# Weight strips of 256 columns, conversions of 768, a half-chunk start and one masked copy per unit, in a kernel of RWKV attention followed by a multiplicative feed-forward

The kernel runs on one core of one Trainium2 chip. The metric is the device time of one execution in microseconds (us). Engines are called as the profile calls them: PE is TensorE, PEld its weight loads, DVE is VectorE, ACT is ScalarE, POOL is GpSimd.

## The reference

```python
# r, k, v: (4, 8, 768, 48) float32; w, u: (8, 48)
for t in range(768):
    cur = einsum('bhd,bhe->bhde', u * k[t], v[t])
    y[t] = einsum('bhd,bhde->bhe', r[t], state + cur)
    state = w * state + einsum('bhd,bhe->bhde', k[t], v[t])
x = y as (3072 tokens, 384)
a, b = x @ w1, x @ w2            # w1, w2: (384, 1024)
out = ((a * b) @ w3) @ w_out     # w3: (1024, 1024), w_out: (1024, 384)
```

The four weight matrices arrive as 64-bit floats, and must be made fp32 on the chip.

## The kernel before

The first part works in 24 units: six chunks of 128 time steps, four batch rows each. A unit scales k and r by powers of w (`krs`, on DVE), transposes them (PE), multiplies all pairs of time steps of each head (`ps_a`, PE), puts the upper triangle into a table `AT` that already holds the diagonal (a masked copy on DVE, the diagonal on ACT), and multiplies the table and the state with v and r (`ps_y`, PE). The four units of a chunk give 512 tokens, in `xT`. The second part works by chunk: for each of eight groups of 128 columns a tile of `abt` is the product of `x @ w1` and `x @ w2` (function `ab`), w3 and w_out are folded into one matrix on the way (`fold`), and `o` multiplies it with the tiles.

A weight piece is converted by one ACT and six DVE instructions, the same for any width:

```python
nc.scalar.activation(out=power, in_=hi.bitcast(F32), func=ABS)
nc.vector.scalar_tensor_tensor(dst, power, 1.125 * 2.0 ** -15, hi.bitcast(F32), ALU.is_ge, ALU.mult)
nc.vector.tensor_scalar(tb, hb, 0x07FFFFFF, 3, ALU.bitwise_and, ALU.logical_shift_left)
nc.vector.scalar_tensor_tensor(hb, hb, 0xC0000000, tb, ALU.bitwise_and, ALU.bitwise_or)
nc.vector.tensor_scalar(pb, hb, 0xFF800000, None, ALU.bitwise_and)      # from here: the low word
nc.vector.scalar_tensor_tensor(t, lo, 2.0 ** -52, power, ALU.mult, ALU.mult)
nc.vector.tensor_add(dst, dst, t)
```

The pairs of a unit use two PSUM tiles of 128 x 512 fp32 (one bank each, as this text calls that size), and two masked copies:

```python
ps = [psA.tile([C, NP, C], F32, tag="a", name=f"ps_a{n}_{i}") for i in range(2)]
for p in range(NP):
    for i in range(2):
        nc.tensor.matmul(ps[i][:, p, :], lhsT=kT[n][rows(i), p, :], rhs=rT[n][rows(i), p, :], ...)
for i in range(2):
    nc.vector.copy_predicated(AT[n][:, i], later.bitcast(I32)[:, None, :].to_broadcast([C, NP, C]), ps[i])
```

The second part is spread over the units by a plan, one list for each chunk; a scheduler then orders the instructions of each engine:

```python
beside = [
    W12[0],                                              # w1, w2: first 512 columns
    merge(W12[1], AB(0, range(KH))) + AB(0, range(KH, KF)),
    merge(AB(1), WO + W3(range(3))),
    merge(AB(2, range(KH)), W3(range(3, KF))) + O(0) + AB(2, range(KH, KF)),
    merge(O(1) + O(2), AB(3)),
    merge(O(3), AB(4)),
]
```

The kernel's PSUM pools hold eight tiles of at most this size, in pairs: two for transposes, two for `ps_a` of the pairs, two for `ps_y` and the states, two for the second part.

## Time and profile before

| | before |
|---|---|
| time, median of 3 runs | 565.74 us (564.63 to 566.33) |
| span of the profiled execution | 562.7 us |
| PE busy, all of it | 539.0 us, 96% |
| first matmul of the second part | 46.53 us |
| last `ps_b` of chunk 0 ends | 109.27 us |
| first matmul of O(0) | 254.7 us |

The last rows of the table are marks for a race: where PE is full, the time at which it reaches a mark says how far one kernel leads the other. The second mark can be read in the timeline of PE (start, length, engine, line, operation): the eighth tile's last group ends where the next unit's transposes start.

```profile
106.69 2.74 PE L408 MATMUL ps_b<-xT,w 128*128 128x512 f32 x6
109.27 0.60 PE L295 MATMUL ps_kT<-ident,krs 128*128 128x128 f32 x4
```

### The profile page before, as it was taken

To read this page: it belongs to the slowest core of one execution; us is meant where nothing else is said; L and a number is where in the kernel's file an instruction comes from. 1 tells how busy PE (TensorE), PEld (TensorE's weight loads), DVE (VectorE), ACT (ScalarE), POOL (GpSimd) and SP (SyncE) were. 2 spreads that over 40 slices of the span, in tenths; PEclk is the share of its full clock that TensorE was granted. 3 is DMA by queue.
4 is the path that set the end of the run, shared out by engine and by line. 5 is a ranking of instruction groups with operands and counts; after the bars stand their busy time and mean duration, and the time that the engine had idled before them with its cause. 6 is when DMAs were issued, how large, how long until landed. Compare 5 with 4: busy or idle time off the path is not lost.

```text
span 562.7 us, 8088 instructions
## 1 busy us (share of the span) xinstructions
PE 539.0 (96%) x3304; PEld 307.2 (55%) x3304; DVE 255.5 (45%) x495; ACT 169.2 (30%) x400; POOL 3.6 (1%) x17
## 2 busy tenths in 40 slices
PE   3869999999999999999999999999999999999996
PEld 2656555455655565565645556555555555544453
DVE  5999999998674696840220414233211100001100
ACT  3745544454433263331211213122132110111010
POOL 2000000000000000000000000000000000000000
PEclk9969999999999999999999999999999999999999
DMA  7956543554233243220110202021010000000001
GB/s 161 227 134 160 153 112 90 149 170 132 43 115 77 76 120 97 57 43 21 50 29 14 57 14 57 15 57 30 16 29 14 1 15 14 29 28 0 0 16 47
DMA packets 84129, 37.52 MB, mean 67 GB/s; under 512 B 76273, under 2 KB 79474, under 8 KB 84082
## 3 DMA queue, kind: packets, MB, share of 16 engines
q1 hardware_dynamic: 84082, 36.91, 25.0%
q8 instruction: 28, 0.46, 0.3%
q14 instruction: 19, 0.16, 0.1%
HBM read 32.18 MB, written 4.72 MB: 66 GB/s over the span
## 4 chain that ended last, share of the span: by engine, by line
PE 90%; DVE 6%; DMA 1%; issue 1%; ACT 1%; SPq 0%; DVEq 0%; ACTq 0%
PE ps_o L414 22%; PE ps_b L408 22%; PE ps_a L403 22%; PE ps_w L267 7%; PE ps_a L307 5%; PE ps_y L363 4%; PE ps_y L355 3%; PE ps_kT L295 2%; PE ps_s L381 2%; PE ps_rT L295 2%; PE ps_w3T L263 1%; DVE t L238 1%; DVE AT L310 1%; DMA raw<-in_moe_w_dram 1%; DVE w L239 1%
## 5 line engine op out<-in xcount | busy, mean ns | idle before, releaser
L403 PE MATMUL ps_a<-xT,w 128*128 128x512 f32 x288 | 133.4, 597 | 0.7 <-DVE w L239 0.7
L409 DVE TENSOR_TENSOR abt<-ps_b,a 128x512 f32<-128x512 f32 x48 | 33.1, 691 | 221.8 <-PE ps_b L408 196.5
L408 PE MATMUL ps_b<-xT,w 128*128 128x512 f32 x288 | 132.5, 594 | 0.1
L414 PE MATMUL ps_o<-w,abt 128*128 128x384 f32 x384 | 127.2, 488 | 0.0
L414 PEld LDWEIGHTS ps_o<-w,abt 128*128 128x128 f32 x384 | 72.0, 190 | 49.2 <-issue 2.0
L408 PEld LDWEIGHTS ps_b<-xT,w 128*128 128x128 f32 x288 | 54.2, 190 | 67.1 <-issue 63.5
L403 PEld LDWEIGHTS ps_a<-xT,w 128*128 128x128 f32 x288 | 52.9, 190 | 56.8 <-issue 50.1
L289 ACT ACTIVATE AT<-ident,dg 128x128 f32<-128x128 f32 x192 | 59.1, 391 | 1.7 <-DVE dg L284 1.7
L405 ACT COPY a<-ps_a 128x512 f32<-128x512 f32 x48 | 28.0, 584 | 104.3 <-PE ps_a L403 104.3
L310 DVE COPY_PREDICATED AT<-later,ps_a 128x512 f32<-128x512 int32 x48 | 33.0, 730 | 31.2 <-PE ps_a L307 30.9
L417 ACT COPY osb<-ps_o 128x384 f32<-128x384 f32 x24 | 11.5, 479 | 108.7 <-PE ps_o L414 85.7
L267 PE MATMUL ps_w<-wo,w3T 128*128 128x384 f32 x128 | 43.1, 490 | 0.0
L307 PEld LDWEIGHTS ps_a<-rT,kT 64*128 64x128 f32 x384 | 25.9, 198 | 19.2 <-issue 11.3
L307 PE MATMUL ps_a<-rT,kT 64*128 64x128 f32 x384 | 31.7, 299 | 2.7 <-ACT rT L298 2.7
L367 ACT COPY xT<-ps_y 128x384 f32<-128x384 f32 x24 | 11.5, 478 | 74.3 <-PE ps_y L363 74.3
L231 ACT ACTIVATE power<-raw 128x512 f32<-128x512 f32 (+1 forms) x36 | 23.6, 655 | 31.5 <-DVE t L238 19.7
L267 PEld LDWEIGHTS ps_w<-wo,w3T 128*128 128x128 f32 x128 | 23.7, 190 | 15.7 <-ACT w3T L264 0.6
L363 PE MATMUL ps_y<-AT,vnat 128*32 128x128 f32 x768 | 29.1, 274 | 2.4 <-DVE AT L310 1.3
L298 ACT COPY kT<-ps_kT 128x512 f32<-128x512 f32 x24 | 14.0, 585 | 40.7 <-PE ps_kT L295 40.7
L363 PEld LDWEIGHTS ps_y<-AT,vnat 128*32 128x32 f32 x768 | 22.4, 110 | 5.2 <-DVE AT L310 2.5
L277 DVE TENSOR_TENSOR krs<-krin,pn_in 128x768 f32<-128x768 f32 x24 | 22.9, 956 | 3.8 <-ACT pn_in L179 2.8
L238 DVE SCALAR_TENSOR_TENSOR t<-raw,power 128x512 f32<-128x512 uint32 (+1 forms) x36 | 23.6, 655 | 0.2
(64 smaller groups left out, 339.1 us busy)
## 6 DMA issues: line engine op xcount, KB each, us to landing
raw<-in_moe_w_dram SPq DMA_DIRECT2D x28, 512.0 KB, 3.6
krin<-in_k_dram SPq DMA_DIRECT2D x24, 192.0 KB, 2.8
krin<-in_r_dram SPq DMA_DIRECT2D x24, 192.0 KB, 3.4
vnat<-in_v_dram SPq DMA_DIRECT2D x24, 192.0 KB, 2.8
out_dram<-osb SPq DMA_DIRECT2D x24, 192.0 KB, 1.9
raw<-in_moe_w_out_dram SPq DMA_DIRECT2D x8, 384.0 KB, 2.9
ub<-in_u_dram SPq DMA_DIRECT2D x1, 192.0 KB, 5.3
wucol<-in_w_dram SPq DMA_DIRECT2D x2, 0.8 KB, 1.9
```

The costliest lines, as they stand in the source:

```text
L231: nc.scalar.activation(out=power, in_=hi.bitcast(F32), func=ABS)
L238: nc.vector.scalar_tensor_tensor(t, lo, 2.0 ** -52, power, ALU.mult, ALU.mult)
L267: nc.tensor.matmul(ps, lhsT=w3T[:, kc, :], rhs=wo[kc], start=(kc == 0), stop=(kc == KF - 1))
L289: nc.scalar.activation(out=AT[n][:, i, p, :], in_=ident, func=COPY, scale=dg[:, h:h + 1])
L307: nc.tensor.matmul(ps[i][:, p, :], lhsT=kT[n][rows(i), p, :], rhs=rT[n][rows(i), p, :], start=True, stop=True)
L310: nc.vector.copy_predicated(AT[n][:, i], later.bitcast(I32)[:, None, :].to_broadcast([C, NP, C]), ps[i])
L363: nc.tensor.matmul(to(q, g), lhsT=vv[:, p, x:x + Q], rhs=AT[n][:, i, p, :], start=(not c and m < P // Q), stop=True, skip_group_check=True)
L403: nc.tensor.matmul(pa, lhsT=w1[:, q, js], rhs=xT[c][:, q, :], start=(q == 0), stop=(q == KM - 1))
L405: nc.scalar.copy(out=a, in_=pa)
L408: nc.tensor.matmul(pb, lhsT=w2[:, q, js], rhs=xT[c][:, q, :], start=(q == 0), stop=(q == KM - 1))
L409: nc.vector.tensor_mul(abt[c, j], pb, a)
L414: nc.tensor.matmul(po, lhsT=abt[c, j][:, b * C:(b + 1) * C], rhs=w34[:, j, :], start=(j == 0), stop=(j == KF - 1))
```

## The change

The intent is to let PE begin the second part earlier, in the stretch where it idles: with weights that are complete in strips of 256 columns, two tiles of chunk 0 can be computed for the first two batch rows before the other two exist. Wider conversions and one masked copy for two shall save DVE instructions. The core of the diff:

```diff
-    NIN, NV, NS, NRAW = 3, 3, 2, 3
+    NIN, NV, NS, NRAW = 3, 4, 2, 3
-    w1 = const.tile([P, KM, DF], F32)
+    w1 = const.tile([P, DF // STRIP, KM, STRIP], F32)      # STRIP = 256; w2 alike
+    ab_pieces = [(dst[:, z], src.rearrange("(q p) n -> p q n", p=P)[:, :, z * STRIP:(z + 1) * STRIP])
+                 for z in range(DF // STRIP) for dst, src in ((w1, moe_w1), (w2, moe_w2))]
...
-    load(0)
+    load(0, "kr")
+    landed = {0: fetch(ab_pieces[0])}
     (ub is loaded here)
-    landed = {0: fetch(ab_pieces[0])}
-    load(1)
+    load(0, "v")
+    load(1, "kr")
     landed[1] = fetch(ab_pieces[1])
+    load(1, "v")
...
-        psA = arm.enter_context(tc.tile_pool(name="psA", bufs=2, space=PSUM))
+        psA = arm.enter_context(tc.tile_pool(name="psA", bufs=1 if fast else 2, space=PSUM))
...
-                ps = [psA.tile([C, NP, C], F32, tag="a", name=f"ps_a{n}_{i}") for i in range(2)]
+                ps = psA.tile([C, 2, NP, C], F32, tag="a", name=f"ps_a{n}")
-                for i in range(2):
-                    nc.vector.copy_predicated(AT[n][:, i], ...to_broadcast([C, NP, C]), ps[i])
+                nc.vector.copy_predicated(AT[n].rearrange("s i p t -> s (i p) t"),
+                                          ...to_broadcast([C, H, C]), ps.rearrange("s i p t -> s (i p) t"))
...
+        def ab(c, j, ts=slice(0, NT)):                       # only the tokens ts; 17 abt tiles, not 20
...
+            [none, none, none, W12[0] + AB(0, range(0, 2), halves[0]), none, W12[1][:1], none,
+             AB(0, range(0, 2), halves[1]) + W12[1][1:] + AB(0, range(2, 4))],
+            [none, W12[2], none, AB(0, range(4, 6)), none, W12[3], none, AB(0, range(6, 8))],
             merge(AB(1), WO + W3(range(3))),
-            merge(AB(2, range(KH)), W3(range(3, KF))) + O(0) + AB(2, range(KH, KF)),
-            merge(O(1) + O(2), AB(3)),
+            merge(AB(2, range(1)), W3(range(3, KF))) + O(0) + AB(2, range(1, KF)),
+            O(1) + merge(O(2), AB(3)),
```

More of the change, by code (lines that the diff above doesn't have):

```diff
@@ L63 @@
     PIECE = 512
+    STRIP = 256
+    RAW = KM * STRIP
     W_LOW, W_HIGH = 0.6, 1.6
@@ L85 @@
     krs = [const.tile([C, 2, H, PAD], F32, name=f"krs{i}") for i in range(NS)]
-    raws = [const.tile([P, PIECE], U64, name=f"raw{i}") for i in range(NRAW)]
+    raws = [const.tile([P, RAW], U64, name=f"raw{i}") for i in range(NRAW)]
     st = [const.tile([P, NP, PD], F32, name=f"st{b}") for b in range(B)]
@@ L100, with load @@
     NU = len(units)
-    def load(n):
+    def load(n, which="krv"):
         if n >= NU:
@@ L106, in load @@
         ts = slice(c * C, (c + 1) * C)
-        nc.sync.dma_start(out=krin[n % NIN][:, 0], in_=k[b, :, ts, :].rearrange("h t d -> t h d"))
-        nc.sync.dma_start(out=krin[n % NIN][:, 1], in_=r[b, :, ts, :].rearrange("h t d -> t h d"))
-        nc.sync.dma_start(out=vnat[n % NV][:, :, :D], in_=v[b, :, ts, :].rearrange("h t d -> t h d"))
-    w1 = const.tile([P, KM, DF], F32)
-    w2 = const.tile([P, KM, DF], F32)
+        for nm, src, dst in (("k", k, krin[n % NIN][:, 0]), ("r", r, krin[n % NIN][:, 1]), ("v", v, vnat[n % NV][:, :, :D])):
+            if nm in which:
+                nc.sync.dma_start(out=dst, in_=src[b, :, ts, :].rearrange("h t d -> t h d"))
+    w1 = const.tile([P, DF // STRIP, KM, STRIP], F32)
+    w2 = const.tile([P, DF // STRIP, KM, STRIP], F32)
     w34 = const.tile([P, KF, DM], F32)
-    ab_pieces = [(dst[:, q, js], src[q * P:(q + 1) * P, js])
-                 for js in (slice(z * PIECE, (z + 1) * PIECE) for z in range(DF // PIECE))
-                 for q in range(KM) for dst, src in ((w1, moe_w1), (w2, moe_w2))]
+    ab_pieces = [(dst[:, z], src.rearrange("(q p) n -> p q n", p=P)[:, :, z * STRIP:(z + 1) * STRIP])
+                 for z in range(DF // STRIP) for dst, src in ((w1, moe_w1), (w2, moe_w2))]
     sent = [0]
@@ L126, in fetch @@
             return None
-        raw = raws[sent[0] % NRAW][:, :src.shape[1]]
+        _, m, n = src.shape
+        raw = raws[sent[0] % NRAW][:, :m * n].rearrange("p (m n) -> p m n", m=m)
         sent[0] += 1
@@ L225, in convert @@
                 return
-            n = src.shape[1]
-            lo, hi = (raw.bitcast(U32).rearrange("p (n z) -> p n z", z=2)[:, :, z] for z in range(2))
-            t, power = (work.tile([P, PIECE], F32, tag="cv", bufs=4, name=nm)[:, :n] for nm in ("t", "power"))
+            _, m, n = src.shape
+            lo, hi = (raw.bitcast(U32).rearrange("p m (n z) -> p m n z", z=2)[:, :, :, z] for z in range(2))
+            t, power = (work.tile([P, RAW], F32, tag="cv", bufs=3, name=nm)[:, :m * n].rearrange("p (m n) -> p m n", m=m)
+                        for nm in ("t", "power"))
             tb, hb, pb = t.bitcast(U32), dst.bitcast(U32), power.bitcast(U32)
@@ L248, in out_weight @@
             wo[c] = work.tile([P, DM], F32, tag="wo", bufs=KF, name=f"wo{c}")
-            weight((wo[c], moe_w_out[c * P:(c + 1) * P, :]))
+            weight((wo[c][:, None, :], moe_w_out[c * P:(c + 1) * P, None, :]))
         def w3_weight(j, z):
@@ L254, in w3_weight @@
             js = slice(z * PIECE, (z + 1) * PIECE)
-            weight((w3n[j][:, js], moe_w3[j * P:(j + 1) * P, js]))
+            weight((w3n[j][:, None, js], moe_w3[j * P:(j + 1) * P, None, js]))
         def fold(j):
@@ L279, in scale @@
                 nc.scalar.copy(out=krs[n % NS][:, :, :, :D], in_=kr)
-            ruk = work.tile([C, H, D], F32, tag="ruk", bufs=2, name=f"ruk{n}")
+            ruk = work.tile([C, H, D], F32, tag="ruk", bufs=1, name=f"ruk{n}")
             dg = work.tile([C, H], F32, tag="dg", bufs=2, name=f"dg{n}")
@@ L302, in pairs @@
             if fast:
-                ps = [psA.tile([C, NP, C], F32, tag="a", name=f"ps_a{n}_{i}") for i in range(2)]
+                ps = psA.tile([C, 2, NP, C], F32, tag="a", name=f"ps_a{n}")
                 for p in range(NP):
                     for i in range(2):
-                        nc.tensor.matmul(ps[i][:, p, :], lhsT=kT[n][rows(i), p, :], rhs=rT[n][rows(i), p, :],
+                        nc.tensor.matmul(ps[:, i, p, :], lhsT=kT[n][rows(i), p, :], rhs=rT[n][rows(i), p, :],
                                          start=True, stop=True)
-                for i in range(2):
-                    nc.vector.copy_predicated(AT[n][:, i], later.bitcast(I32)[:, None, :].to_broadcast([C, NP, C]), ps[i])
+                nc.vector.copy_predicated(AT[n].rearrange("s i p t -> s (i p) t"),
+                                          later.bitcast(I32)[:, None, :].to_broadcast([C, H, C]),
+                                          ps.rearrange("s i p t -> s (i p) t"))
                 return
@@ L396, in body @@
         abt = {}
-        def ab(c, j):
-            abt[c, j] = work.tile([P, NT], F32, tag="abt", bufs=2 * KF + KF // 2, name=f"abt{c}_{j}")
-            js = slice(j * P, (j + 1) * P)
+        def ab(c, j, ts=slice(0, NT)):
+            if (c, j) not in abt:
+                abt[c, j] = work.tile([P, NT], F32, tag="abt", bufs=2 * KF + 1, name=f"abt{c}_{j}")
+            z, js = j * P // STRIP, slice(j * P % STRIP, j * P % STRIP + P)
+            n = ts.stop - ts.start
             pa = psF.tile([P, NT], F32, tag="f", name=f"ps_a{c}_{j}")
             for q in range(KM):
-                nc.tensor.matmul(pa, lhsT=w1[:, q, js], rhs=xT[c][:, q, :], start=(q == 0), stop=(q == KM - 1))
+                nc.tensor.matmul(pa[:, :n], lhsT=w1[:, z, q, js], rhs=xT[c][:, q, ts], start=(q == 0), stop=(q == KM - 1))
             a = work.tile([P, NT], F32, tag="sa", bufs=2, name=f"a{c}_{j}")
-            nc.scalar.copy(out=a, in_=pa)
+            nc.scalar.copy(out=a[:, :n], in_=pa[:, :n])
             pb = psF.tile([P, NT], F32, tag="f", name=f"ps_b{c}_{j}")
             for q in range(KM):
-                nc.tensor.matmul(pb, lhsT=w2[:, q, js], rhs=xT[c][:, q, :], start=(q == 0), stop=(q == KM - 1))
-            nc.vector.tensor_mul(abt[c, j], pb, a)
+                nc.tensor.matmul(pb[:, :n], lhsT=w2[:, z, q, js], rhs=xT[c][:, q, ts], start=(q == 0), stop=(q == KM - 1))
+            nc.vector.tensor_mul(abt[c, j][:, ts], pb[:, :n], a[:, :n])
         def o(c, b):
@@ L419, in o, with AB @@
             nc.sync.dma_start(out=out[row:row + C, :], in_=osb)
-        def AB(c, js=range(KF)):
-            return [lambda c=c, j=j: ab(c, j) for j in js]
+        def AB(c, js=range(KF), ts=slice(0, NT)):
+            return [lambda c=c, j=j: ab(c, j, ts) for j in js]
         def O(c):
@@ L431, in first @@
             convert(ab_pieces[i], landed[i])
-        half = len(ab_pieces) // 2
-        W12 = [[lambda i=i: first(i) for i in range(z * half, (z + 1) * half)] for z in range(2)]
+        W12 = [[lambda i=i: first(i) for i in (2 * z, 2 * z + 1)] for z in range(DF // STRIP)]
         WO = [lambda c=c: out_weight(c) for c in range(KF)]
@@ L446, in body @@
         KH = KF // 2
+        halves = [slice(0, NT // 2), slice(NT // 2, NT)]
+        none = []
         beside = [
-            W12[0],
-            merge(W12[1], AB(0, range(KH))) + AB(0, range(KH, KF)),
+            [none, none, none, W12[0] + AB(0, range(0, 2), halves[0]), none, W12[1][:1], none,
+             AB(0, range(0, 2), halves[1]) + W12[1][1:] + AB(0, range(2, 4))],
+            [none, W12[2], none, AB(0, range(4, 6)), none, W12[3], none, AB(0, range(6, 8))],
             merge(AB(1), WO + W3(range(3))),
-            merge(AB(2, range(KH)), W3(range(3, KF))) + O(0) + AB(2, range(KH, KF)),
-            merge(O(1) + O(2), AB(3)),
+            merge(AB(2, range(1)), W3(range(3, KF))) + O(0) + AB(2, range(1, KF)),
+            O(1) + merge(O(2), AB(3)),
             merge(O(3), AB(4)),
@@ L461, in body @@
         for c in range(NCH):
-            done = 0
+            plan = beside[c]
+            if not isinstance(plan[0], list):
+                cuts = [len(plan) * m // (2 * B) for m in range(2 * B + 1)]
+                plan = [plan[cuts[m]:cuts[m + 1]] for m in range(2 * B)]
             for b in range(B):
@@ L465, in body @@
                 load(n + 2)
-                steps = []
                 if n + 1 < NU:
-                    steps += [lambda: (scale(n + 1), turn(n + 1))]
-                steps += [lambda: (n + 1 < NU and pairs(n + 1), output(n), update(n))]
-                for i, step in enumerate(steps):
+                    scale(n + 1)
+                    turn(n + 1)
+                for step in plan[2 * b]:
                     step()
-                    due = len(beside[c]) * (b * len(steps) + i + 1) // (B * len(steps))
-                    while done < due:
-                        beside[c][done]()
-                        done += 1
+                if n + 1 < NU:
+                    pairs(n + 1)
+                output(n)
+                update(n)
+                for step in plan[2 * b + 1]:
+                    step()
         for step in tail:
```

## The prediction

> **What bounds the kernel now.** I read the whole-page summary first: it says which engine is full over the span and where it is not.
>
> ```profile
> span 562.7 us, 8088 instructions
> ...
> PE 539.0 (96%) x3304; PEld 307.2 (55%) x3304; DVE 255.5 (45%) x495; ACT 169.2 (30%) x400; POOL 3.6 (1%) x17
> ...
> PE   3869999999999999999999999999999999999996
> ...
> DVE  5999999998674696840220414233211100001100
> ...
> PEclk9969999999999999999999999999999999999999
> ```
>
> PE is full in nearly every slice of 14 us; only the first three slices and the last one fall short. So the change can only win in the first 47 us, or must be judged by whether it opens new holes later. The row of DVE shows the other limit: DVE is full from the second slice to about 125 us, just where PE is not. PEclk dips in the third slice. Then I cut the span into five stretches (start:end, length, then busy us of PE, PEld, DVE, ACT, POOL with counts, clock, DMA share, GB/s).
>
> ```profile
> 0.00:12.00 12.00, 2.19 (x10) 1.85 (x11) 6.56 (x33) 3.32 (x5) 3.58 (x17) 1.00 0.75 153
> 12.00:47.00 35.00, 26.82 (x337) 20.89 (x337) 32.01 (x62) 20.48 (x56) 0.00 (x0) 0.85 0.76 180
> 47.00:104.00 57.00, 56.23 (x444) 30.36 (x443) 56.34 (x111) 29.02 (x74) 0.00 (x0) 1.00 0.50 129
> 104.00:250.00 146.00, 145.76 (x1011) 85.65 (x1010) 110.52 (x213) 58.93 (x134) 0.00 (x0) 1.00 0.35 97
> 250.00:562.70 312.70, 307.95 (x1507) 168.44 (x1506) 50.05 (x80) 57.45 (x134) 0.00 (x0) 1.00 0.09 25
> ```
>
> PE idles 9.8 us before 12 us, 8.2 us between 12 and 47, 0.8 and 0.2 us in the next two stretches. DVE has 0.7 us free in 47:104, but 35 us free in 104:250. The view of waits of PE names the releasers, and the timeline shows that busy time flatters the start: the same 16 pair products take 2.08 us at 38.07 us and 1.16 us at 43.05 us.
>
> ```profile
> PE ps_p L178 <- DVE both L172: 8.0, 1, 8.0
> PE ps_kT L295 <- DVE krs L277: 4.0, 3, 1.8
> PE ps_a L307 <- ACT rT L298: 2.7, 1, 2.7
> PE ps_y L363 <- DVE AT L310: 1.3, 3, 0.9
> ...
> PE ps_w3T L263 <- DVE w3n L239: 0.2, 1, 0.2
> ```
>
> ```profile
> 38.07 2.08 PE L307 MATMUL ps_a<-rT,kT 64*128 64x128 f32 x16 [2.69 <-ACT rT L298]
> ...
> 43.05 1.16 PE L307 MATMUL ps_a<-rT,kT 64*128 64x128 f32 x16
> 46.53 1.12 PE L403 MATMUL ps_a<-xT,w 128*128 128x512 f32 x2
> ```
>
> The last line is the first matmul of the second part. Counting PE's work before it at dense rates from the timeline (transposes 0.88 us a unit, pairs 1.1, y of the first chunk 1.0, state product 0.6, table transposes 0.88): 0.88 + 5 x 0.88 + 5 x 1.1 + 4 x 1.0 + 4 x 0.6, with 0.8 for the first state read, is 18.0 us in 46.5 us. PE has thus lost 28.5 us there. Some 12 us go before any input and table is ready, so some 16.5 us are what an earlier start of the second part could aim at.
>
> [...] From start to start in the timeline a two-input instruction took 0.47 us at 384 elements, 0.60 at 512 and 0.87 at 768, thus about 1.04 ns an element and 0.07 us fixed[...]; the trace has 0.33 us for the 512-element bit mask[...].
>
> **The change, part by part.** (1) Wider conversion pieces. One of 512 is six DVE instructions, 4 x 0.60 + 2 x 0.33 = 3.07 us, and there are 12 for w1 and w2: 36.8 us. One of 768 is 4 x 0.87 + 2 x 0.47 = 4.40 us, and there are 8: 35.2 us. DVE saves 1.6 us, all in its full stretch. w_out and w3 keep their sizes. (2) One copy_predicated of 1024 columns for two of 512: 1.24 us from start to start become about 1.14. Seven or eight units lie in the full stretch: 0.7 us. The price is that the next unit's pair products wait for the whole copy; they lie far enough apart. (3) The first strips of w1 and w2 are complete after two pieces (8.8 us of DVE) where the old order needed six (18.4 us) for 512 columns. Tiles 0 and 1 of chunk 0 can then start on the first two batches: 4 groups of 3 matmuls with 256 columns, about 5.1 us of PE work moved forward, and as much with the other half once unit 3 is done. PE's columns stay equal, as a group of six passes takes 2.58 us at 512 columns. The splitting adds only 12 products and two short DVE multiplies (4 x 0.33 against 2 x 0.60, +0.1 us). (4) A first strip loaded early. It puts 786 KB instead of 524 KB ahead of the second unit's k and r, whose r already kept DVE waiting 0.5 us; 0.26 MB at the 180 GB/s of the second stretch is 1.4 us more wait. The fourth v tile lets v loads go sooner; no wait of DVE or PE on v stands in the waits. (5) Later chunks: w3's last five rows now go beside one tile of chunk 2 instead of four. PE has less to do beside them, so DVE must keep up.
>
> Now DVE's queue in the changed order, from 10.65 us (its first krs), up to the last conversion of w2: krs 8 x 0.87 = 7.0; the three ruk/dg instructions of nine units and two of a tenth, 13.6; seven copy_predicated, 8.0; state updates of six units (0.7 each, and 0.47 twice), 5.1; eight conversions, 35.2; four half multiplies and four full ones, 3.7. The sum is 72.6 us, with 2 us of waiting for the second unit's input: 85.3 us. In the kernel before, the last w2 conversion ended at 91.1 us, but with an extra krs, copy_predicated and state update before it (3.3 us). DVE as such gains only 2 to 3 us; the order does the rest. Up to the krs of unit 8 come 5.3 us more (w_out's first piece, a ruk pair, a dg, a copy, a state update, the krs): 90.6 us. PE must wait for this krs, as the order has the transposes of unit 8 ahead of the tail of tiles 6 and 7. I get some 2 us of PE idleness there and as much for unit 6 at 68 to 70 us. Behind it PE has 13 us of work: 0.9 transposes, 0.4 y, 1.1 pairs, 0.6 state, 1.8 rest of a, three more groups of 2.7[...]. Chunk 0's eighth tile is thus done at about 105 us. In the kernel before, the timeline puts this end at 109.3 us, with the same units done. **The lead is about 4 us**, not the 16.5 of the idle time, because DVE, which makes every operand that PE would use, stays full.
>
> From there both are bound by PE. In the w3 stretch I set the changed order side by side: each row needs 2 x 3.07 = 6.1 us of DVE and 0.88 + 16 x 0.32 = 6.0 us of PE. DVE has to interleave units of 4.6 us. Three shared buffers for w3 rows and their transposes let a row start only when a fold two before is done. My sums give PE small waits at the last two rows, 0 to 1.5 us together. The later order of O(1), O(2) and AB(3) has full PE on both sides: zero. Seventeen abt tiles instead of twenty suffice, as O(0) ends before the eighteenth is written. Sum: 4 gained, about 0.8 given back: 3.2 us, 565.7 - 3.2 = 562.5 us.
>
> **The rivals.** (a) PE's holes close fully: up to 16 us, 550 us. For it speaks the size of the hole; against it DVE's nearly full row up to 125 us. It needs the half-chunk work to land exactly in waits that otherwise stay empty, and the units not to be held up. (b) The half-chunk work couples DVE's strict order to PE early: DVE's multiplies wait for cold matmuls, the recurrence slips, and the lead vanishes: 565 to 568 us. The clock view with 0.85 between 12 and 47 us speaks for it; against it, my tallies leave 0.5 to 2 us between PE's end and DVE's turn at most places. (c) DVE becomes the bound in the w3 stretch, having lost three tiles' worth of cover (15.6 us of PE): up to 5 us of waits on w3n, so 566 us. Against it stand DVE's 35 us free in 104:250. (d) The larger first strip delays unit 1: at most 2 us, 564.
>
> **Range and chances.** Centre 562.5. Up to 6 us of further gain if the waits for units 6 and 8 vanish; 4 to 5 us the other way if (b) or (c) come true. I take 556.5 to 566.5. Two per cent is 11.3 us: faster by so much needs two thirds of the whole hole, 0.05; slower by so much has no cause that I see, 0.02.
>
> **What would show it.** The first 256-column ps_a should start near 28 us and the first full one near 51; chunk 0's last ps_b should end at 103 to 107 us. PE idle in 12:47 should fall, but new waits of kT on krs should stand between 60 and 95 us, about 4 us. Conversion rows should read near 0.95 us at 768 (start to start 0.87) and copy_predicated near 1.25 us. Waits of ps_w3T on w3n should stay under 2 us. I am wrong if DVE has idle time of more than 3 us before 85 us, if the first O matmul comes after 240 us (at 254.8 before, less three tiles, 239 without a lead), or if PE waits for w3n by more than 3 us.

Cut from the text: one term of the sum, 1.5 us of PE for switches and a slow start, an estimate for which no measured numbers were given. With it the sum was 90.6 + 12.9 + 1.5 = 105.0 us for the end of chunk 0's eighth tile, the "about 105" that stands; without it, it comes to 103.5, a lead of 5.8 us and not "about 4", and a forecast of some 561 us and not 562.5. Three figures of parts 1 to 3 are for shapes that the kernel before does not have, and can be worked out from the rates in the text (1.04 ns an element and 0.07 us fixed; 0.33 us for the mask of 512): 0.47 us for the mask of 768 columns ((0.33 - 0.07) x 1.5 + 0.07 = 0.46), 1.14 us for the copy of 1024 (1.13) and 0.33 us for the multiply of 256 (0.34). They are estimates; the measured values are 0.47, 1.19 and 0.33 us. "Cold" means matmuls at a low granted clock: in the kernel before, the clock was 0.50 from 38.07 to 40.10 us, where the 16 pairs took 2.08 us, and 1.00 from 43.05 to 44.20 us, where they took 1.16.

## The result

The changed kernel took 563.12 us in the median of four runs (562.22 to 563.47), the kernel before 565.77 (564.63 to 566.33) beside it. The ratio is 0.9953, with an interval of 0.9933 to 0.9973. Ratios here are the mean time of one kernel's runs over that of the other's of the same rounds, so not quite the ratio of the medians. The gain of 2.65 us is real, as the interval lies below 1. The whole-page summary of the kernel after, to be read against the prediction's first fence:

```profile
span 560.0 us, 8068 instructions
...
PE 536.6 (96%) x3328; PEld 310.4 (55%) x3328; DVE 256.5 (46%) x449; ACT 168.9 (30%) x398; POOL 3.7 (1%) x18
...
PE   2879999999999999999999999999999999999997
...
DVE  6989999998765979520320304233111100001100
...
PEclk9889999999999999999999999999999999999999
```

PE's third slice is fuller, and DVE is about as full as before. The clock is better in the third slice (8 for 6) and lower in the second (8 for 9). By stages (start:end, length, busy us of PE, PEld, DVE, ACT, POOL with counts, clock, DMA share, GB/s):

```profile
12.00:47.00 35.00, 28.60 (x323) 22.78 (x323) 32.40 (x52) 21.62 (x58) 0.00 (x0) 0.90 0.87 195
47.00:104.00 57.00, 54.66 (x490) 33.15 (x489) 56.52 (x95) 27.96 (x69) 0.00 (x0) 1.00 0.50 124
104.00:250.00 146.00, 144.94 (x1019) 87.21 (x1018) 109.30 (x198) 57.95 (x133) 0.00 (x0) 1.00 0.36 98
```

PE's idle time fell from 8.2 to 6.4 us between 12 and 47 us, and rose from 0.8 to 2.3 and from 0.2 to 1.1 us in the next two stretches. What PE waits for (us in total, times, longest):

```profile
PE ps_kT L300 <- DVE krs L282: 5.1, 5, 1.8
PE ps_a L312 <- DVE AT L314: 2.2, 1, 2.2
PE ps_a L312 <- ACT AT L294: 2.1, 1, 2.1
PE ps_w3T L268 <- DVE w3n L244: 1.1, 2, 0.6
```

The first and last lines I had expected. The two in the middle are new: pairs that wait for a table `AT`. Pairs do not read `AT`; what they need is the PSUM tile that the copy into `AT` empties. The view puts one of them down to ACT, which wrote diagonals of a later table at that moment; but the wait ended at 19.50 us, 0.14 us after the end of the masked copy (18.07 to 19.36 us in DVE's timeline), so I read it as a wait for the copy as well. The timeline of PE shows the other wait, and the marks:

```profile
26.88 1.56 PE L411 MATMUL ps_a<-xT,w 128*128 128x256 f32 x6
...
33.86 1.12 PE L312 MATMUL ps_a<-rT,kT 64*128 64x128 f32 x8 [2.16 <-DVE AT L314]
34.91 2.79 PE L416 MATMUL ps_b<-xT,w 128*128 128x256 f32 x6
37.54 1.46 PE L411 MATMUL ps_a<-xT,w 128*128 128x256 f32 x6
...
92.91 0.66 PE L300 MATMUL ps_kT<-ident,krs 128*128 128x128 f32 x4 [1.07 <-DVE krs L282]
...
103.79 2.74 PE L416 MATMUL ps_b<-xT,w 128*128 128x512 f32 x6
...
236.92 13.49 PE L422 MATMUL ps_o<-w,abt 128*128 128x384 f32 x41
```

The second part starts at 26.88 us and not at 46.53. But at 33.86 PE has stood still for 2.16 us, and the group after it takes 2.79 us, where the same six matmuls take 1.46 three microseconds later: the clock had dropped (0.53 granted between 33.86 and 37.50 us, 1.00 from there to 40.00). DVE's timeline shows both ends of the knot:

```profile
32.43 1.29 DVE L314 COPY_PREDICATED AT<-later,ps_a 128x1024 f32<-128x1024 int32 x1
...
37.74 0.42 DVE L417 TENSOR_TENSOR abt<-ps_b,a 128x256 f32<-128x256 f32 x1 [1.39 <-PE ps_b L416]
...
91.89 0.96 DVE L282 TENSOR_TENSOR krs<-krin,pn_in 128x768 f32<-128x768 f32 x1
```

The masked copy ends at 33.72 us and lets PE go at 33.86; PE's slow group then makes DVE, the engine that is full, wait 1.39 us at 37.74. The last line is the krs of unit 8, for which PE waits at 92.91.

The marks: chunk 0 ends at 106.37 us (103.79 and 2.58), 2.9 us ahead of the kernel before. The first O matmul starts at 236.92; before it was 254.7 (the prediction's 254.8 is from the view of the critical chain), less three tiles of 2 x 2.58 us that now come after it, 239.2, thus 2.3 us ahead. The spans differ by 2.7 us. So the whole gain is made before 106 us, and neither lost nor added to later.

### The profile page after: what moved, and what is told of

Its sections match the earlier page's. It is cut to its first block, busy times and chain, and to the rows that moved or that the text cites. A ratio compares the mean times of both kernels' runs of the same rounds, so it can differ in the third digit from the quotient of the medians.

```text
span 560.0 us, 8068 instructions
## 1 busy us (share of the span) xinstructions
PE 536.6 (96%) x3328; PEld 310.4 (55%) x3328; DVE 256.5 (46%) x449; ACT 168.9 (30%) x398; POOL 3.7 (1%) x18
## 4 chain that ended last, share of the span: by engine, by line
PE 83%; DVE 12%; issue 2%; DMA 1%; SPq 1%; ACT 0%; DVEq 0%; ACTq 0%
PE ps_o L422 22%; PE ps_b L416 20%; PE ps_a L411 20%; PE ps_w L272 6%; PE ps_a L312 4%; PE ps_y L369 3%; PE ps_y L361 2%; PE ps_s L387 2%; PE ps_kT L300 1%; PE ps_rT L300 1%; DMA krin<-in_r_dram 1%; DVE t L243 1%; PE ps_w3T L268 1%; DVE w L244 1%; DVE w L237 1%
## 5 line engine op out<-in xcount | busy, mean ns | idle before, releaser
L417 DVE TENSOR_TENSOR abt<-ps_b,a 128x512 f32<-128x512 f32 (+1 forms) x50 | 33.5, 670 | 222.8 <-PE ps_b L416 197.0
L411 PE MATMUL ps_a<-xT,w 128*128 128x512 f32 (+1 forms) x300 | 133.8, 580 | 0.4 <-ACT xT L373 0.4
L416 PE MATMUL ps_b<-xT,w 128*128 128x512 f32 (+1 forms) x300 | 133.3, 581 | 0.2 <-DVE abt L417 0.2
L416 PEld LDWEIGHTS ps_b<-xT,w 128*128 128x128 f32 x300 | 57.5, 193 | 67.7 <-issue 64.3
L411 PEld LDWEIGHTS ps_a<-xT,w 128*128 128x128 f32 x300 | 55.2, 190 | 55.4 <-issue 50.9
L413 ACT COPY a<-ps_a 128x512 f32<-128x512 f32 (+1 forms) x50 | 28.4, 568 | 114.2 <-PE ps_a L411 114.0
L314 DVE COPY_PREDICATED AT<-later,ps_a 128x1024 f32<-128x1024 int32 x24 | 31.6, 1316 | 20.0 <-PE ps_a L312 19.8
L236 ACT ACTIVATE power<-raw 128x512 f32<-128x512 f32 (+2 forms) x32 | 22.8, 711 | 37.1 <-DVE w3n L244 16.6
L243 DVE SCALAR_TENSOR_TENSOR t<-raw,power 128x512 f32<-128x512 uint32 (+2 forms) x32 | 23.1, 722 | 0.5
```

What stands on the lines that cost most here:

```text
L314: nc.vector.copy_predicated(AT[n].rearrange("s i p t -> s (i p) t"), later.bitcast(I32)[:, None, :].to_broadcast([C, H, C]), ps.rearrange( ...
L411: nc.tensor.matmul(pa[:, :n], lhsT=w1[:, z, q, js], rhs=xT[c][:, q, ts], start=(q == 0), stop=(q == KM - 1))
L413: nc.scalar.copy(out=a[:, :n], in_=pa[:, :n])
L416: nc.tensor.matmul(pb[:, :n], lhsT=w2[:, z, q, js], rhs=xT[c][:, q, ts], start=(q == 0), stop=(q == KM - 1))
L417: nc.vector.tensor_mul(abt[c, j][:, ts], pb[:, :n], a[:, :n])
```

## The experiments

Twelve kernels were run in three calls. The kernel before ran beside each, with medians of 565.97, 564.75 and 564.79 us, so I compare ratios and give both. The changed kernel was timed in a call of its own, e1, e2, e6 and e7 together in one call on one chip, the others in two calls on another chip.

| kernel | median us | ratio to before | interval | profiled span |
|---|---|---|---|---|
| changed kernel | 563.12 | 0.9953 | 0.9933 to 0.9973 | 560.0 |
| e1: two pair tiles, two copies | 559.00 | 0.9874 | 0.9856 to 0.9892 | 557.2 |
| e2: no half chunks | 562.97 | 0.9945 | 0.9929 to 0.9960 | 560.6 |
| e10: e1 without half chunks | 561.50 | 0.9942 | 0.9922 to 0.9963 | 559.8 |
| e12: before, one copy | 564.55 | 0.9996 | 0.9979 to 1.0014 | 561.8 |
| e6: changed, light conversion | 559.20 | 0.9879 | 0.9859 to 0.9900 | 557.4 |
| e7: before, light conversion | 557.61 | 0.9849 | 0.9829 to 0.9870 | 556.2 |
| e11: e1, light conversion | 557.04 | 0.9861 | 0.9841 to 0.9882 | 555.2 |
| e9: strips converted in thirds | 565.89 | 1.0022 | 1.0005 to 1.0039 | 562.3 |
| e3: e1, old order of loads | 559.88 | 0.9909 | 0.9892 to 0.9927 | 558.5 |
| e4: e1, three v tiles | 559.11 | 0.9901 | 0.9881 to 0.9921 | 556.8 |
| e5: before, late plan | 565.63 | 1.0012 | 0.9995 to 1.0029 | 563.7 |
| e13: e1, two multiplies on POOL | 581.11 | 1.0275 | 1.0252 to 1.0298 | 579.3 |

The theory: DVE is full up to about 90 us (in the changed kernel it is busy for 56.5 of the 57 us from 47 to 104) and sets when PE gets its operands, so the gain is small, and the merged masked copy takes part of it back, through the pair tile. The rivals: the half-chunk start itself is worthless, or DVE's amount of work does not matter.

### e1: undo the merged copy

```diff
-        psA = ...(name="psA", bufs=1 if fast else 2, ...)
+        psA = ...(name="psA", bufs=2, ...)
-                ps = psA.tile([C, 2, NP, C], F32, tag="a", ...)
+                ps = [psA.tile([C, NP, C], F32, tag="a", ...) for i in range(2)]
-                nc.vector.copy_predicated(<all 1024 columns>)
+                for i in range(2):
+                    nc.vector.copy_predicated(AT[n][:, i], ..., ps[i])
```

> The changed kernel with the old pair products: two one-bank tiles and two copies of 512 columns for each unit, the rest of the change kept. Theory: in the changed kernel the one pair tile made PE wait 2.1 us at 17.4 us and 2.2 us at 31.7 us for the copy of the unit before, and [...]the next 256-column group took 2.63 instead of about 1.4 us. With two tiles the wait at 31.7 us goes, and the time falls by 1 to 2 us to about 561.5. Rival: DVE is the bound of this stretch; two copies cost it 0.05 to 0.1 us more for each unit, 0.5 us up to unit 8, and the waits on PE were slack: 563 to 564. The order of the queues may shift as well; I look for the 256-column ps_b at half clock in the timeline.

It took 559.00 us, ratio 0.9874, against 0.9953 with the merged copy. The difference of the ratios is 4.5 us; the medians differ by 4.1, the means of all spans by 3.7 (557.1 and 560.8). The two intervals do not touch. One part undone is thus worth more than the whole change had gained, and e1 beats both kernels. Its timeline of PE:

```profile
32.43 0.41 PE L368 MATMUL ps_y<-AT,vnat 128*32 128x128 f32 x4 [1.24 <-DVE AT L315]
...
34.68 0.93 PE L312 MATMUL ps_a<-rT,kT 64*128 64x128 f32 x10
35.62 1.56 PE L415 MATMUL ps_b<-xT,w 128*128 128x256 f32 x6
...
90.18 0.65 PE L300 MATMUL ps_kT<-ident,krs 128*128 128x128 f32 x4 [1.44 <-DVE krs L282]
```

At 32.43 PE waits too, but 1.24 us and not 2.16, the group that took 2.79 us takes 1.56 (the mean clock from 12 to 47 us is 0.95, against 0.90), and DVE has no wait for it: in the view of waits, DVE waits 0.2 us in all between 17 and 90 us, in the changed kernel 2.2. Unit 8 is reached at 90.18 and not at 92.91.

What waits at 32.43 is not the same work, though. It is the y matmuls, which read the table; in e1 they stand ahead of the next pairs, which start at 34.68 without a wait. DVE's timeline has the two copies 0.8 us earlier than the one copy of the changed kernel (32.43), and y starts when the first of them is done:

```profile
31.64 1.34 DVE L315 COPY_PREDICATED AT<-later,ps_a 128x512 f32<-128x512 int32 x2
```

So the edit changed the order of the queues along with the tile, and the share of each is not separated. Nor did it end every wait of the pairs: both forms give one unit the same two banks, and at 18.68 us the pairs of e1 still wait 1.8 us for a copy (2.1 in the changed kernel).

By the transposes of unit 5 e1 leads by 1.4 us (62.25 and 63.69 us), which goes with DVE's saved waits; the other 1.3 us come between there and unit 8, where the scheduler put fewer instructions of later units ahead of unit 8's krs (one pair of `ruk` multiplies and one w_out instruction less). That this order is the cause of the second 1.3 us is an inference. Also open is whether one wide copy out of two such tiles would do as well; no run tried it.

### e12: the merged copy in the kernel before

```diff
(on the kernel before)
-        psA = ...(name="psA", bufs=2, ...)
+        psA = ...(name="psA", bufs=1 if fast else 2, ...)
-                ps = [psA.tile([C, NP, C], F32, tag="a", ...) for i in range(2)]
+                ps = psA.tile([C, 2, NP, C], F32, tag="a", ...)
-                for i in range(2):
-                    nc.vector.copy_predicated(AT[n][:, i], ..., ps[i])
+                nc.vector.copy_predicated(<all 1024 columns>)
```

> The kernel before with one pair tile of two banks and one copy of 1024 columns, nothing else. Theory: the shared tile costs PE its waits in the first 47 us in this kernel too, because the pair products of unit n+1 are issued before or just after the copy of unit n: 1 to 4 us slower, 567 to 570. Rival: without half-chunk groups behind the pair products PE has nothing to lose there, and DVE saves 0.05 us a unit: 565 to 566.

The ratio is 0.9996. In the kernel before, the merged copy costs nothing and saves nothing. PE waits as long as 3.2 us for a copy there, but what waits is y, which reads the table; no pairs wait for the pair tile in this run, as y stands ahead of them in PE's queue:

```profile
19.93 1.08 PE L364 MATMUL ps_y<-AT,vnat 128*32 128x128 f32 x32 [3.19 <-DVE AT L309]
```

Also, the second part begins only at about 46 us in that kernel, so that the wait holds up none of it. That this is why nothing is lost is my reading; what the run shows is that the loss belongs to the combination.

### e2 and e10: no half chunks, with one pair tile and with two

```diff
-            [none, none, none, W12[0] + AB(0, range(0, 2), halves[0]), none, W12[1][:1], none,
-             AB(0, range(0, 2), halves[1]) + W12[1][1:] + AB(0, range(2, 4))],
+            [none, none, none, W12[0], none, W12[1][:1], none,
+             AB(0, range(0, 2)) + W12[1][1:] + AB(0, range(2, 4))],
```

> The changed kernel without the half-chunk start: tiles 0 and 1 of chunk 0 are computed whole after unit 3, everything else kept. Theory: the first halves (four groups, 5.1 us of PE work at full clock) fill holes of PE that DVE leaves before 47 us, and two later waits for krs give part back; without them the end moves by 2 to 4 us, to 565 to 567, so that the half-chunk start is nearly the whole gain. Rival: the gain comes from the strips and the cheaper conversions, which let the second part start earlier anyway, and the early halves only delay the recurrence: 562 to 564.

> Two pair tiles and two copies (as e1) and no half-chunk start (as e2). In e2 the half start was worth nothing (562.97 against 563.1), but there the pair tile held PE up. Theory: the half start is worth its moved work once the pair products no longer wait; without it the time is 2 to 4 us above e1's 559.0, 561 to 563. Rival: DVE's queue is full anyway and decides when w1 and w2 are ready, so the half start is worth nothing here as well: 558.5 to 559.5, and the gain of e1 is that of the strips and the cheaper conversions.

With the single pair tile, the half-chunk start is worth nothing: 0.9945 without it, 0.9953 with it. With two tiles it is worth 3.8 us by ratio: 0.9942 without it, 0.9874 with it (2.5 us by the medians). Read the other way, the merged copy costs nothing by ratio where there are no half chunks (0.9945 in e2, 0.9942 in e10; 1.5 us by the medians), although the pairs of e2 wait 1.9 and 2.2 us for it as in the changed kernel. By ratio, then, it is not these waits as such that cost, but what stands behind them. The timeline of PE in e10 shows what fills the gap in e1:

```profile
37.35 0.41 PE L368 MATMUL ps_y<-AT,vnat 128*32 128x128 f32 x4 [1.82 <-issue]
...
38.70 1.92 PE L368 MATMUL ps_y<-AT,vnat 128*32 128x128 f32 x28
```

Where e1 has three groups of 256 columns, from 35.62 to 39.7 us, e10 stands still for 1.82 us and then runs slowly (1.92 us for 28 y matmuls, 1.07 in e1 at 33.37). Slow matmuls do not follow every wait: after the 1.82 us here they were slow from 37.70 us on (14 state products took 1.08 us, 0.67 at 32.47), and after the 2.16 us in the changed kernel as well (2.79 us above), but after one of 2.38 us in e10 (before 28.55 us) four transposes took 0.66 us, as they do without a wait (0.65 at 25.08 us). What decides this is not shown.

### e6, e7, e11: half of the conversion left out

```diff
-        def convert(piece, raw):
+        def convert(piece, raw, light=False):
...
+            if light:
+                return                # after the third DVE instruction: the low word is not added
...
-            convert(ab_pieces[i], landed[i])
+            convert(ab_pieces[i], landed[i], light=True)       # w1 and w2 only
```

These kernels are less exact on purpose; the comparison with the reference still accepted them. They are no replacements. They take 8 x (0.47 + 0.87 + 0.87) = 17.7 us from DVE in the new form (e6, e11), and 12 x (0.33 + 0.60 + 0.60) = 18.4 us in the old (e7).

> The changed kernel with the conversion of w1 and w2 cut to its first three DVE instructions (the low words of the doubles are not added; the weights lose their last bits on purpose, the time is what is wanted). DVE has 8 x 2.2 = 17.6 us less to do before 87 us. Theory (DVE, not PE or the start, limits how much of PE's hole can be filled): the time falls by 6 to 12 us, to 551 to 557, as PE finds its operands earlier. Rival (the hole is made of the start, of cold clocks and of the chain of a unit through PE, ACT and DVE): it falls by less than 3 us.

> The same cut in the kernel before: 12 x 1.53 = 18.4 us less DVE work before 91 us. If DVE alone sets the early stage in both, it gains about as much as the changed kernel does with the cut (6 to 12 us) and the distance of the two stays near 2.7 us. If the old order (second part only after the whole first chunk) is the limit of the kernel before, it gains clearly less, 2 to 5 us, and the distance grows to 6 us or more: then the change's order is worth more the less DVE has to do.

> e1 with the light conversion of e6 (low words not added on purpose). In e6 the cut of 17.6 us of DVE work brought only 3.9 us, in the kernel before (e7) 8.4 us. Theory: in e6 the pair tile and ACT's diagonal tiles held PE; with two tiles DVE's load is the limit again and the cut brings 5 to 9 us against e1: 550 to 554. Rival: what limits e6 is the chain of a unit (ACT's eight diagonal writes, krs), not the tile: the cut brings 2 to 4 us, 555 to 557.

In the kernel before, the lighter load brought 8.5 us (1.0 to 0.9849), in the changed one 4.2 (0.9953 to 0.9879), in e1 only 0.7 by ratio, and 2.0 in spans. For e6 and e11 I had expected more (6 to 12 and 5 to 9 us). So DVE's work is a strong limit of the kernel before. That it is a weaker one of the changed kernel and of e1 is not shown, because most of the relief did not reach the point that counts. DVE's timelines list 37 instructions of w_out's conversion ahead of unit 8's krs in e6 and 34 in e11, against 3 in the changed kernel, 2 in e1 and 1 in e7. From start to start they take about 15 and 13.5 us, so that only some 4 to 5 of the 17.7 us left this part of the queue; the krs starts at 89.68 us in e6 and at 91.89 in the changed kernel. How many of these instructions only filled time in which DVE would have waited was not separated.

With the light conversion the change shows no gain: e6 is 1.6 us slower than e7, with intervals that just overlap, and e11 does not differ from e7 beyond the noise. In e6 the pair tile comes forward again. The timelines of PE and of DVE:

```profile
20.01 2.08 PE L314 MATMUL ps_a<-rT,kT 64*128 64x128 f32 x16 [3.17 <-ACT AT L296]
```

```profile
18.57 1.29 DVE L316 COPY_PREDICATED AT<-later,ps_a 128x1024 f32<-128x1024 int32 x1
```

The pairs wait 3.17 us and start 0.15 us after the end of the masked copy; again the releaser named is ACT, and again the time fits the copy. ACT had written the diagonals of the copy's table by 17.66 us; the copy started 0.9 us later, behind a `ruk` multiply that had waited 0.31 us for r.

In e11, ACT itself waits for the raw strips to land, in the view of waits from 12 to 47 us; the DMA share is 0.98 there (0.91 in e1, 0.76 in the kernel before):

```profile
ACT power L236 <- DMA raw<-in_moe_w_dram: 3.4, 2, 2.4
```

How much the order of DVE's queue, the pair tile and the loads each take was not separated.

### e9: more DVE work

```diff
-            convert(ab_pieces[i], landed[i])
+            dst, src = ab_pieces[i]
+            for q in range(KM):
+                convert((dst[:, q:q + 1], src[:, q:q + 1]), landed[i][:, q:q + 1])
```

> The changed kernel with each strip converted in three pieces of 256 columns: 48 more pairs of instructions in sum 8 x 12 = 96 more DVE instructions, each with some 0.07 us fixed cost: 6.4 us more DVE work before 88 us. If DVE's load is the limit there, the time rises by nearly all of it, 4 to 6.5 us, to 567 to 569.5, ratio about 1.004 (the mirror image of e6, whose cut of 17.6 us gave 3.9). If PE's waits on the pair tile hide DVE's load, it rises by less than 2 us, ratio under 0.999.

Each strip is converted in three pieces of 256, so 96 DVE instructions are added. From start to start, one of 256 columns takes 0.335 us in this run (26.17 to 26.51, 26.51 to 26.85, 27.32 to 27.65 us), and one of 768 in the changed kernel 0.87: three for one cost 0.135 us more, 0.067 for each added, which is 6.4 us for 96. The ratio rose from 0.9953 to 1.0022, 3.9 us (2.8 by the medians). More DVE work costs about 0.6 of itself (0.4 by the medians), so the changed kernel is not free of DVE. The edit also adds 16 instructions to ACT, and the queues' order differs again: no pairs wait for a copy in this run, y does (3.6 us).

### e3, e4, e5: the early load, the fourth v tile, the late plan

```diff
(e3, on e1)
-    load(0, "kr")
-    landed = {0: fetch(ab_pieces[0])}
+    load(0)
     (ub is loaded here)
-    load(0, "v")
-    load(1, "kr")
+    landed = {0: fetch(ab_pieces[0])}
+    load(1)
     landed[1] = fetch(ab_pieces[1])
-    load(1, "v")
(e4, on e1)
-    NIN, NV, NS, NRAW = 3, 4, 2, 3
+    NIN, NV, NS, NRAW = 3, 3, 2, 3
(e5, on the kernel before)
-            merge(AB(2, range(KH)), W3(range(3, KF))) + O(0) + AB(2, range(KH, KF)),
-            merge(O(1) + O(2), AB(3)),
+            merge(AB(2, range(1)), W3(range(3, KF))) + O(0) + AB(2, range(1, KF)),
+            O(1) + merge(O(2), AB(3)),
```

> e1 with the first loads in the old order: k, r, v of unit 0, u, first strip, k, r, v of unit 1, second strip. My prediction held that the early strip delays unit 1 by 1.4 us; the trace of the changed kernel shows DVE's krs of unit 1 at 12.19 us against 12.57 before, as the v loads moved behind. Theory now: the new order costs nothing and may save up to 1 us, so that the old one is 0 to 1 us slower than e1 (ratio 0.987 to 0.989). Rival (the prediction): the old order is faster by about 1 us, ratio 0.985.

> e1 with three v tiles. With three, the load of v for unit n+3 waits in SP's queue for the state product of unit n, and all loads behind it wait as well, raw strips among them; the DMA engines are at 0.91 of their time in 12:47 in e1. Theory: the fourth tile keeps SP's queue moving where PE runs late; without it a raw strip or k and r come 1 to 2 us later, ratio 0.989 to 0.991. Rival: loads are early enough, nothing changes: 0.987 to 0.988.

> The kernel before with only the later part of the change's plan: one tile of chunk 2 instead of four beside w3's last rows, and O(1) before the mix of O(2) and AB(3). Theory: PE stays full in both orders, the small waits for w3n go from 0.2 to about 1 us as they did in the changed kernel, ratio 0.999 to 1.002. Rival: DVE cannot keep up with w3 without the cover of three tiles: 3 to 5 us slower, 1.005 or more.

With the old order of loads the krs of unit 1 starts at 12.93 us after a wait of 0.9 us for its k and r; in the changed kernel it starts at 12.19 without one. The other runs agree: 12.14 to 12.39 us in the eight kernels with the new order (e13 aside), 12.55 to 13.07 in the five with the old. The time is unclear: e3's ratio 0.9909 and e1's 0.9874 come from different calls, and beside e4, e3 was 0.8 us slower in the median with intervals that overlap. I put the early load at about 1 us at most. The fourth v tile did nothing: 559.11 against 559.00 us, and PE's waits agree to 0.2 us. The wait that e4's expectation names is there with three v tiles and with four: SP's queue waits for the state product 16 times in the kernel before, 73.2 us in all (from 24.53 to 28.41 us, for one, it issues nothing and then a load of v), and 15 times in the changed kernel, 95.8 us. The late plan alone did nothing, 1.0012 with an interval that holds 1.

### e13: take work from DVE another way

```diff
(on e1)
-            nc.vector.tensor_mul(ruk, kr[:, 0], kr[:, 1])
-            nc.vector.tensor_mul(ruk, ruk, ub)
+            nc.gpsimd.tensor_mul(ruk, kr[:, 0], kr[:, 1])
+            nc.gpsimd.tensor_mul(ruk, ruk, ub)
```

> e1 with the two ruk multiplies of each unit on the Pool engine, which is idle after 4 us: DVE loses 2 x 0.47 us for each unit, 8.5 us by unit 8, results unchanged. If DVE's load is the limit in e1, the time falls by 2 to 5 us to 554 to 557 and this beats both kernels. Rival: the Pool multiply takes longer and stands in the chain dg, diagonal tiles, copy, y of each unit[...], and nothing is gained or some us are lost: 559 to 563.

This failed, at 581.11 us. The groups of POOL (out<-in, shapes and count, then busy us and mean ns of one, then its idle time) and PE's waits:

```profile
L287 POOL TENSOR_TENSOR ruk<-krin 128x384 f32<-128x384 f32 x24 | 28.0, 1168 | 326.2 <-DMA krin<-in_r_dram 250.4 <-DVE t L243 31.9 <-DVE t L239 13.9
```

```profile
PE ps_a L312 <- DVE AT L315: 8.6, 1, 8.6
```

A multiply takes 1.17 us on POOL and 0.55 on DVE. PE waited 8.6 us for one copy, and its clock between 12 and 47 us was 0.76. The slower multiplies are not what made that wait: those of unit 0 were done on POOL at 12.67 us. Their sum `dg` stood behind nine conversion instructions in DVE's queue, ACT waited for a raw strip until 22.22, and its diagonals began only at 23.02, so that the copy started at 25.64. The timelines also show what I had overlooked: at 29.02 us, beside a POOL multiply (28.32 to 29.97), DVE's 768-column mask takes 1.37 us, where those at 14.39 and 16.73 us take 0.56 and 0.55. The runs show the slowing, not its cause.

```profile
20.64 0.55 DVE L289 TENSOR_REDUCE dg<-ruk 128x8 f32<-128x384 f32 x1
...
23.02 4.77 ACT L294 ACTIVATE AT<-ident,dg 128x128 f32<-128x128 f32 x16
...
28.32 1.65 POOL L287 TENSOR_TENSOR ruk<-krin 128x384 f32<-128x384 f32 x1 [0.67 <-DVE dg L289]
...
29.02 1.37 DVE L239 TENSOR_SCALAR t<-w 128x768 uint32<-128x768 uint32 x1
```

Over the whole kernel the 48 multiplies that left DVE had taken 26.7 us in e1, but DVE's busy time fell only from 256.9 to 254.5 us, so its other instructions took 24 us longer. The masked copies out of PSUM kept their 0.73 us. Nearly the whole relief was thus lost on DVE itself; how much of the 22 us is due to this and how much to the order of the queues was not separated.

## Why the prediction was right or wrong

The time was right: 562.5 us predicted, 563.12 measured, inside the range. That it came so close is in part luck. The merged copy was counted among DVE's savings, 0.7 us, and cost about 4; the rest of the change gained 7.0 us by the medians (e1, 565.97 to 559.00), where the sum of 3.2 without those 0.7 leaves 2.5. Two errors of 4 to 5 us met with opposite signs. The reason given for a small gain, that DVE makes every operand and stays full, held for the kernel before (e7) and in part for the changed one (e9; e6 does not decide it). The step that failed is this one of part 2: "The price is that the next unit's pair products wait for the whole copy; they lie far enough apart."

- **The merged copy.** They do not lie far enough apart: two waits of 2.1 and 2.2 us, a group at a granted clock of 0.53 and 1.4 us of DVE's time. Undoing the merge gains about 4 us (e1), of which some 1.3 us came with a different order of the queue. The loss shows only where half-chunk groups stand behind such waits: e2 and e12 lose nothing by ratio. The saving was mis-sized too. From start to start one copy of 1024 columns takes 1.19 us and two of 512 took 1.24, so 0.05 us a unit and not 0.10. The trade was 0.4 us of DVE for eight units against 4 us. Rival (b), DVE coupled to PE's slow matmuls, thus came true in part, and I had taken it as an alternative where it was a deduction.
- **The half-chunk start.** "About 5.1 us of PE work moved forward" is right in kind: the first 256-column group started at 26.88 us (28 expected), the first of 512 at 53.39 (51). With two pair tiles it is worth 3.8 us by ratio, 2.5 by the medians (e1, e10), with one it is worth nothing (e2). The prediction had no term for such an interaction.
- **DVE's queue.** w2's last conversion ended at 87.4 us (85.3 expected), unit 8's krs at 92.85 (90.6). The sum of durations was sound to about 1.3 us: up to the first of these ends 76.8 us passed from 10.65 us on, 2.9 of them idle, against 72.6. The 2 us of waiting booked for unit 1's input did not come; the 2.9 came elsewhere, 1.4 of them in the point above. Conversion rows read 0.95 us at 768 columns, 0.87 from start to start, as expected, and the bit masks 0.55 and 0.47. The masked copy reads 1.32 us (near 1.25 expected). The 2.9 us of idle time are just under the 3 that would have counted against me; in e1 it is 1.3.
- **The marks.** Chunk 0 ended at 106.37 us (105 expected), a lead of 2.9 and not 4. The waits of transposes for krs at 71.95 and 92.91 us are 2.1 us and not 4: a mis-sized term, and in the good direction.
- **After chunk 0.** The waits for w3 rows are 1.1 us (0 to 1.5 expected), and O starts at 236.92 (under 240). The late plan gave nothing, as expected (e5). A check of this came free: from the end of unit 8's krs to the end of the span, the changed kernel needs 467.15 us, e1 467.07, e2 467.11, e10 467.04 and e11 467.04. Whatever differs among these kernels is decided before 93 us. (e6 needs 466.8 us; e9, with more conversion pieces, 468.4, and does not fit.)
- **The early strip.** "0.26 MB at the 180 GB/s of the second stretch is 1.4 us more wait" had the wrong sign: unit 1's krs started 0.38 us earlier than before (12.19 and 12.57 us), and the other runs bear this out (see e3). I had counted the strip that moves forward and not the v loads that move back.
- **Rivals.** PE's hole did not close (a), and DVE did not become the bound among the w3 rows (c). For (d) see the early strip.

The best kernel is the change without the merged copy (e1), with 559.0 us against 563.1 and 566.0.

## What to carry to other kernels

Before merging two small reads of PSUM into one, ask who waits for the halves: here both forms use the same two banks for a unit, but in halves the first bank and the first half of the table are free after 0.73 us (the mean copy of 512 columns in e1), and as one only after 1.32 (the mean of 1024 in the changed kernel). The saving of one copy's fixed cost (0.05 us here, 1.24 less 1.19) stands against that, and against what the scheduler makes of it. Parts of a change can cancel: test each part alone and with the others, as the half-chunk start was worth 0 or 3 to 4 us depending on a buffer elsewhere. Where an engine is full, what counts is which of its instructions come before the one that the next engine waits for, not the sum of its work: in e6 most of the work taken off was replaced there by other work (only some 4 to 5 of the 17.7 us left that part of the queue).
